# A Fourier mixer and gated layer on one core: quarter-array products in issue order, and eleven forward units beside the first chunk

## The chip, the cores and the metric

The kernel runs on 1 core of one Trainium2 chip. The metric is the device time of one execution in microseconds (us). The kernel before takes 2664.31 us, the median of 3 runs (2664.19 to 2669.71). Lower is better.

## What is computed

The input is 8 sequences of 3008 tokens with 256 channels. A real Fourier transform along the sequence, a complex 256 x 256 product per frequency with a bias, a soft threshold and the inverse transform give 24064 tokens of 256 channels. These pass a gated layer of width 1536. The gated layer's weights arrive as 64-bit floats.

```python
def _attn_ref(x, w_r, w_i, b_r, b_i):
    X = np.fft.rfft(x, axis=1)
    Xr, Xi = (X.real.astype(np.float32), X.imag.astype(np.float32))
    Yr = Xr @ w_r - Xi @ w_i + b_r
    Yi = Xr @ w_i + Xi @ w_r + b_i
    lam = 0.01
    Yr = np.sign(Yr) * np.maximum(np.abs(Yr) - lam, 0.0)
    Yi = np.sign(Yi) * np.maximum(np.abs(Yi) - lam, 0.0)
    y = np.fft.irfft(Yr + 1j * Yi, n=x.shape[1], axis=1)
    return y.astype(np.float32)

def _moe_ref(x, w_gate, w_val, w_out):
    gate = 1.0 / (1.0 + np.exp(-(x @ w_gate)))
    val = x @ w_val
    return (gate * val @ w_out).astype(np.float32)
```

## The kernel before

**The transform.** 3008 is 47 x 64, so each sequence (called a batch) is transformed in two steps. Forward step A works with 47-point products: a unit of it is one `products_a` (L207-218), called by `fwd_a` for a full tile `xf` or by `halves_a` (L238-249) for two half tiles `xfh`. Each unit has four products of 47 rows by 64 columns with 512 moving columns. Each lies in one 64 x 64 quarter of the TensorE array: the input half `j` sets the row half, the output half `c` sets the column half. The profile lists each as two instructions, so a unit shows as x8. The results are copied out of PSUM and stored to a buffer `zd` in DRAM. Forward step B (`fwd_b`, L287-312) reads it back as `zf`, makes 64-point products into `pb`, and splits them into `xsf`, `xsh`, `xsl` on ScalarE and VectorE. `mix` (L318-342) multiplies those with the complex weights into `pm`, adds the bias and thresholds. Inverse step B (`inv_b`, L361-379) writes `vz` to a buffer `vd`. Inverse step A (`inv_a`, L401-430) reads `vf` from there: a unit has 32 products of 48 rows by 64 columns with 47 moving columns, again each in one quarter of the array (`j` is the row half, `e` the column half), 64 instructions in the profile. It yields tokens, which stay on the chip as `yth`, `ytl` for the first nine chunks of 512 tokens and go to `yd` in DRAM for the rest.

**The gated layer.** `ffn1` and `ffn2` (L474 to L511) do one of 12 slices `f` of the layer for one chunk `c`: 12 products into `pg` and `pv`, a sigmoid `sg`, a product of both on VectorE (L482), `hh` and `hl`, and 6 products into `po`. Nine chunks are done so, 108 units. The remaining 38 pairs of chunks are done in the kernel's last part by another scheme with fewer products; that part is not touched by the change.

**The order of the work.** Batches go in groups of 1, 1, 2, 2, 2. Up to the end of the first chunk the order is written out by hand (`tc.manual_schedule`): batch 0 is transformed first, then the 12 units of chunk 0 run, and beside them stand 16 units of forward step A for the third group (list `beside`, function `halves`): one before f=0, then one for each f, with a second at f=3, f=9 and f=11. Also in this chunk the 64-bit weights are turned into pairs of 32-bit numbers, one part per unit: SyncE loads `raw` (`load_part`, L953), and ScalarE and VectorE run a chain of small operations on it (L931 to L939), called from `converting` (L446-461), which hangs in a list `hook` as long as the hand-written part lasts.

After it, a scheduler orders the instructions, and a list `side` says what stands beside which unit of the gated layer: `merge` interleaves streams, and each unit of the gated layer takes so much of the side work, by weight, that `side` ends 20 units before unit 108. The first phase of `side` has the transform of the second group with the first 5 of the 16 forward units of the fourth group (`a3[:n]`); the second phase has the transform of the third group with the other 11 (`a3[n:]`). Then `behind_last`: 16 inverse units of the last group in the last 20 units of the gated layer.

**Buffers.** Tiles stand in rings. `xfh` is in a ring of four that is named r2k, `azh` (the output of a half unit) in a ring of four named st, `xf` and `raw` share a ring of six, `vf` has two and one more, and PSUM has a ring of six banks for these products. Loads of `x`, `raw`, `zf`, `vf` go through SyncE's queue (SP); the half units' stores (`zd<-azh`) go through GpSimd's queue (POOL).

Of the kernel before, what the change touches and what calls it, by code (L numbers as in the profile page):

```python
# [9 lines left out]
F32 = mybir.dt.float32  # L10
# [37 lines left out]
WARM_Z, WARM_V = 10, 1  # L48
EARLY = 4
AT_FIRST = 1  # L50
NCONV = 6


# [68 lines left out]
def tile_fft_mix_ffn(ctx: ExitStack, tc, x, w_r, w_i, b_r, b_i, w_one, w_out, mf, mi, mis, fa, fb, mf0, fa0, out):  # L122
# [36 lines left out]
    def r2k(name):  # L159
        gap("gap_r", 192)  # L160
        return p2.tile([P, 2, D], F32R, tag="r2k", bufs=NR2K, name=name)
# [21 lines left out]
    def move(queue, sb, dram, store=False):  # L183
        for j in range(2):
            t = sb[64 * j:64 * j + NQ]
            queue.dma_start(*((dram[j], t) if store else (t, dram[j])))
# [15 lines left out]
    def load_a(b, h):  # L202
# [4 lines left out]
            move(nc.sync, xf, xv[b, h])  # L207
        held["x", b, h] = xf

    def products_a(xs, outs, copies):  # L210
        pa = [bank("pa") for _ in range(2)]
        xs = [t[:, 2 * c:2 * c + 2] if t.shape[1] == 4 else t for c, t in enumerate(xs)]
        for j in (1, 0):
            rows = slice(64 * j, 64 * j + R2)
            for c in (1, 0):
                nc.tensor.matmul(pa[j][64 * c:64 * c + 64], fa_sb[rows], xs[c][rows], start=True, stop=True)
        for copy, o, t in zip(copies, outs, pa):
            copy(o, t.rearrange("p (h c) -> p h c", h=2))

# [16 lines left out]
            move(queue, held.pop(("x", b, h)), zv[b][h], True)  # L236

    def load_half(b, h):  # L238
        xf = r2k("xfh").bitcast(F32)
        move(nc.sync, xf, xv[b, h // 2, :, :, h % 2 * 2:h % 2 * 2 + 2])  # L240
        held["xh", b, h] = xf

    def halves_a(b, u):

        xs = [held.pop(("xh", b, 2 * u + c)) for c in range(2)]
        az = [p2.tile([P, 2, D], F32, tag="st", bufs=NST, name="azh") for _ in range(2)]
        products_a(xs, az, (nc.scalar.copy, nc.scalar.copy))
        for j in range(2):
            move(nc.gpsimd, az[j], zv[b][u, :, :, 2 * j:2 * j + 2], True)


    def load_mf(q, table=mf):
# [148 lines left out]
    def inv_a(u):  # L401
        vf = held.pop(("v", u))
        pa = [bank("pia")[:, :CT * UT].rearrange("p (c k) -> p c k", c=CT) for _ in range(2)]
        for h in range(4):
            for ct in range(CT):
                for j in range(2):
                    rows = slice(64 * j, 64 * j + NQ)
                    for e in range(2):
                        ch = ct * P + 64 * e
                        nc.tensor.matmul(pa[j][64 * e:64 * e + 64, ct, h * R2:(h + 1) * R2], vf[rows, h, ch:ch + 64],  # L410
                                         fb_sb[rows, :R2], start=True, stop=True)
        first = 2 * u * UT // CW
        for j, py in enumerate(pa):
            lo, k = (2 * u + j) * UT, 0
            while k < UT:
                at = lo + k
                c, place = divmod(at, CW)
                n = UT - k if at >= T0 else min(UT - k, CW - place)
                y = py[:, :, k:k + n]
                if at >= T0:  # L420
                    t = result("yf")[:, :CT * n].rearrange("p (c k) -> p c k", c=CT)
                    nc.scalar.copy(t, y)
                    nc.sync.dma_start(yd[:, :, at - T0:at - T0 + n], t)
                elif c == first:
                    split_y(c, place, n, y)
                else:
                    if place == 0:
                        held["carry", c] = p3.tile([P, CT, 384], F32, name="carry", bufs=1), 0
                    t = held["carry", c][0]
                    nc.scalar.copy(t[:, :, place:place + n], y)  # L430
                    held["carry", c] = t, place + n
                k += n
# [79 lines left out]
                nc.sync.dma_start(out[ct * P:(ct + 1) * P, c * CW:(c + 1) * CW], ot)  # L512


    def fft_units(bs, ms):


        aa = [(b, h) for b in bs for h in range(R1 // 8)]
        units = []

        def step_a(i):
            if i == 0:
                for k in range(min(PRE, len(aa))):
                    load_a(*aa[k])
            if i + PRE < len(aa):
                load_a(*aa[i + PRE])
            fwd_a(*aa[i])
            store_a(*aa[i])

        def loads(q, b):  # L530
            if b == bs[0]:
                if q == 0:
                    ms[0, 0] = load_mf(0)
                if q + 1 < NP:
                    ms[q + 1, 0] = load_mf(q + 1)
                if 0 <= q - 1 < NP and (q - 1, 1) not in ms:
                    ms[q - 1, 1] = load_mi(q - 1, False)
            if q == 0:
                load_b(b, 0)
            if q + 1 < NP:  # L540
                load_b(b, q + 1)

        def step(q, b):
            loads(q, b)
            if q < NP:
                fwd_b(b, q, ms[q, 0], False)
            if 0 <= q - 1 < NP:
                mix(b, q - 1)
            if 0 <= q - 2 < NP:
                inv_b(b, q - 2, ms[q - 2, 1], False)  # L550

        first = [(1.0, lambda i=i: step_a(i)) for i in range(len(aa))]
        for q in range(NP + 2):
            wt = 0.9 * (q < NP) + 2.0 * (0 <= q - 1 < NP) + 0.7 * (0 <= q - 2 < NP)
            units += [(wt, lambda q=q, b=b: step(q, b)) for b in bs]
        return first, units
# [433 lines left out]
    nc.vector.memset(ebias, -896.0 * 2.0 ** 23)  # L990
    nc.vector.memset(lam_sb, -LAM)
    mfs, mis_ = {}, {}
    beside = [(b, u) for b in groups[2] for u in range(na)]
    waiting = list(beside)

    def convert(q):
# [26 lines left out]
    def halves(upto):  # L1023

        while waiting:
            i = len(beside) - len(waiting)
            if i >= upto:
                break
            halves_a(*waiting.pop(0))
            if i + NR2K // 2 < len(beside):  # L1030
                load_halves(*beside[i + NR2K // 2])

    with tc.manual_schedule():
        for h in range(na):
# [63 lines left out]
    with tc.manual_schedule():  # L1098
        for u in own0:
            load_v(u)  # L1100
        load_part()
        for h in range(EARLY, na):
            store_a(1, h)
        for bu in beside[NR2K // 2:NR2K // 2 + AT_FIRST]:
            load_halves(*bu)
        for f in range(NF):
            ffn[f]()
            if parts:
                load_part()
            if f in (2, 3):  # L1110
                tables[f - 2, 1] = load_mi(f - 2, False, later=True)
            if f in (5, 6):
                keep_mi(f - 5)
            halves(AT_FIRST + f + 1 + (f > 2) + (f > 8) + (f > 10))
    hook.clear()


# [32 lines left out]
    def merge(*streams):  # L1150
# [2 lines left out]
                                         enumerate(streams) for i, u in enumerate(s)), key=lambda t: t[:2])]  # L1153

    (a3, q3), (a4, q4) = (fft_units(g, {}) for g in groups[3:])
    n = len(a3) // 3
    side = (merge((second_fft, 0, 1), (a3[:n], 0.2, 1)) +
            merge((third_fft, 0, 1), (a3[n:], 0, 0.85), *behind(groups[1])) +
            merge((q3, 0, 1), *in_twos(a4, groups[2])) +
            merge((q4, 0, 1), *behind(groups[3])))  # L1160
    behind_last = sum(inverse(groups[4]), [])
# [104 lines left out]
```

## Time and profile before

| | |
|---|---|
| Median of the runs | 2664.31 us (2664.19 to 2669.71) |
| The profiled execution's own time | 2665.18 us |
| Its span | 2663.2 us, mean granted TensorE clock 0.996 |
| TensorE busy | 2627.3 us, 99% of the span |
| VectorE, ScalarE, GpSimd busy | 1941.7, 1816.8, 1094.1 us |
| Hand-written part, batch 0 | up to about 106 us |
| First chunk of the gated layer | about 106 to 190 us |
| Chunks 1 to 8 beside the transform | about 190 to 918 us |
| `behind_last` | about 918 to 1009 us |
| Last part, untouched | about 1009 to 2663 us |

All times in the views are counted from the start of the span. A row of a timeline gives the start, the duration, the engine, the line, the operation, what it writes and reads, how many instructions stand together (x8), and in brackets the idle time of its engine just before it with what ended that. Matmuls overlap in the pipeline, so what a matmul costs is the distance from its start to the next start, not its duration. "SPq" and "POOLq" are the two queues that issue transfers.

### The profile page before, as it was taken

Reading aid. Unit: us, or ns where it says so; the run is one execution under the profiler, and the core shown is the slowest. Engines: PE = TensorE matmul, PEld = TensorE weight load, DVE = VectorE, ACT = ScalarE, POOL = GpSimd, SP = SyncE. Lnnn points to the kernel's source line nnn. Section 1 sums busy time; section 2 is a strip of 40 time slices with the busy share of each in tenths; the row PEclk is TensorE's granted clock in tenths of the full one; section 3 lists DMA queues with packets and bytes.
Section 4 is the critical chain, followed back from the end, with each engine's and each line's share of the span. In section 5 each row is a group of like instructions: output and inputs, shape, how many; then the busy total and the mean of one; then the engine's idle time right before and its main releaser. Section 6 shows DMA issues by size and latency. Waiting matters only on the chain. (4 is left out here: it accounts for less than half of the span.)

```text
span 2663.2 us, 60273 instructions
## 1 busy us (share of the span) xinstructions
PE 2627.3 (99%) x24032; PEld 2456.9 (92%) x24032; DVE 1941.7 (73%) x3468; ACT 1816.8 (68%) x3530; POOL 1094.1 (41%) x1399
## 2 busy tenths in 40 slices
PE   8999999999999999999999999999999999999998
PEld 6668888888899878999999999999999999999998
DVE  4768778777777525777777777777777777777777
ACT  4666655656565435777777777777777777777776
POOL 0241031123500002555555555555555555555554
PEclk9999999999999999999999999999999999999999
DMA  9887655777655572111111211111111211111111
GB/s 282 259 249 201 189 153 170 195 226 221 198 161 150 175 222 76 33 41 34 39 41 35 47 32 42 33 41 34 40 41 33 46 31 45 33 41 33 40 41 27
DMA packets 200969, 268.27 MB, mean 101 GB/s; under 512 B 19760, under 2 KB 152368, under 8 KB 200688
## 3 DMA queue, kind: packets, MB, share of 16 engines
q1 hardware_dynamic: 179600, 220.04, 28.1%
q0 software_dynamic: 20832, 44.31, 7.8%
q8 instruction: 189, 3.10, 0.5%
q14 instruction: 92, 0.75, 0.1%
q10 hardware_dynamic: 256, 0.07, 0.0%
HBM read 137.33 MB, written 127.01 MB: 99 GB/s over the span
## 5 line engine op out<-in xcount | busy, mean ns | idle before, releaser
L764 POOL TENSOR_TENSOR hs<-gh,xh 128x256 f32<-128x256 f32 x227 | 253.1, 1115 | 734.6 <-DVE gh L754 734.6
L754 DVE TENSOR_TENSOR gh<-gh,pa 128x256 f32<-128x256 f32 x228 | 96.1, 421 | 344.4 <-ACT gh L749 344.4
L713 PE MATMUL pd<-xop,th 128*128 128x256 f32 x1824 | 333.0, 276 | 0.8 <-DVE pc L757 0.8
L713 PE MATMUL pa<-xop,w1h 128*128 128x256 f32 x1824 | 332.6, 276 | 0.0
L713 PEld LDWEIGHTS pd<-xop,th 128*128 128x128 f32 x1824 | 274.5, 188 | 1.7 <-DVE pc L757 1.4
L713 PEld LDWEIGHTS pa<-xop,w1h 128*128 128x128 f32 x1824 | 274.6, 188 | 0.1
L713 PE MATMUL pd<-xop,tl 128*128 128x256 f32 x912 | 251.8, 276 | 0.0
L713 PE MATMUL pa<-xop,w1l 128*128 128x256 f32 x912 | 251.7, 276 | 0.0
L784 DVE TENSOR_TENSOR hpS<-hs,hpS 128x768 fp32r<-128x768 f32 x228 | 217.1, 952 | 0.4 <-ACT hpS L780 0.4
L733 ACT COPY pd<-pb 128x512 f32<-128x512 f32 x228 | 130.0, 570 | 107.8 <-PE pb L713 107.8
L757 DVE TENSOR_TENSOR pb<-pb,m 128x512 f32<-128x512 f32 x228 | 159.5, 699 | 42.3 <-PE pb L713 42.3
L327 PE MATMUL pm<-w_sb,xsh 128*128 128x256 f32 x1008 | 185.9, 286 | 4.1 <-ACT xsh L310 3.1
L780 ACT CAST hpS<-hs 128x768 fp32r<-128x768 f32 x228 | 189.5, 831 | 0.2 <-DVE hs L770 0.2
L729 PE MATMUL acc<-hpS,w2h 128*128 128x256 f32 x912 | 177.5, 276 | 0.0
L733 ACT COPY pb<-pa 128x512 f32<-128x512 f32 x228 | 130.0, 570 | 68.1 <-PE pa L713 68.0
L770 POOL TENSOR_TENSOR hs<-xh,hs 128x256 f32<-128x256 f32 x227 | 168.0, 740 | 17.8
L768 POOL TENSOR_TENSOR gh<-gh 128x256 f32<-128x256 f32 x227 | 167.3, 737 | 17.8
L713 PEld LDWEIGHTS pd<-xop,tl 128*128 128x128 f32 x912 | 171.2, 188 | 0.0
L713 PEld LDWEIGHTS pa<-xop,w1l 128*128 128x128 f32 x912 | 171.2, 188 | 0.0
L766 POOL TENSOR_TENSOR hs<-hs,gh 128x256 f32<-128x256 f32 x227 | 168.1, 741 | 0.0
L713 PE MATMUL pb<-xop,th 128*128 128x256 f32 x912 | 166.5, 276 | 0.0
L713 PE MATMUL pb<-xop,w1h 128*128 128x256 f32 x912 | 166.4, 276 | 0.0
(218 smaller groups left out, 8738.4 us busy)
## 6 DMA issues: line engine op xcount, KB each, us to landing
zf<-zd SPq DMA_DIRECT2D x96, 256.0 KB, 4.3
vf<-vd SPq DMA_DIRECT2D x128, 192.0 KB, 4.1
vd<-vz SPq DMA_DIRECT2D x85, 256.0 KB, 3.1
ypair<-yd SPq DMA_DIRECT2D x38, 512.0 KB, 3.6
yd<-yf SPq DMA_DIRECT2D x103, 188.0 KB, 3.8
out_dram<-ev SPq DMA_DIRECT2D x149, 128.0 KB, 1.8
out_dram<-ev POOLq DMA_DIRECT2D x37, 512.0 KB, 5.8
xf<-in_x_dram SPq DMA_DIRECT2D x80, 192.0 KB, 4.4
```

What stands on the lines that cost most here:

```text
L327: nc.tensor.matmul(o, l, r, start=(i == 0), stop=(i == len(mms) - 1))
L713: nc.tensor.matmul(o[:, i * HW:(i + 1) * HW], l, r, start=start, stop=l is wl, skip_group_check=True)
L729: nc.tensor.matmul(o, l, r, start=(p, b) not in begun, stop=l is wl, skip_group_check=True)
L733: nc.scalar.copy(to, o)
L754: nc.vector.tensor_mul(g, g, o[:, HW:])
L757: nc.vector.tensor_add(to, o, hx[k, "m5"])
L764: e.tensor_add(hx[k, "S"][:, 0], g[:, 1], x[:, 1])
L766: e.tensor_sub(hx[k, "S"][:, 1], hx[k, "S"][:, 0], g[:, 0])
L768: e.tensor_sub(g[:, 1], g[:, 0], g[:, 1])
L770: e.tensor_sub(hx[k, "S"][:, 2], x[:, 0], hx[k, "S"][:, 1])
L780: nc.scalar.copy(t[:, 0], parts_of(k, what))
L784: sub(t[:, 1], parts_of(k, what), t[:, 0])
```

## The change

Three things are changed.

First, a function `behind_last_of` ties the products of one 47-point unit together: after the hand-written part, each but the first must stand behind the TensorE instruction issued before it. It is a tie in order alone; nothing waits on a semaphore for it. It is used in `products_a` and `inv_a`. In `inv_a` the row halves are now taken as `j` = 1, 0.

Second, 11 instead of 16 units of forward step A stand beside the first chunk, one before f=0 and one for each of f=0 to 9. They work in place: the results are copied from PSUM back into the tiles that were loaded, and stored from there. Units 0, 1, 4, 5, 8, 9 use the ring r2k, units 2, 3, 6, 7, 10 the ring st (named `xfs` there). Loads go three units ahead instead of two.

Third, the other five units (`late`) run as full tiles in the first phase of `side`, where the five units of the fourth group stood, and the second phase has all 16 of that group.

```diff
+NHALF = 11
...
+    def behind_last_of(row, ins):
+        if row and not hook:
+            tc.keep_in_program_order(ins)
+        row.append(ins)
+
     def products_a(xs, outs, copies):
...
-                nc.tensor.matmul(pa[j][64 * c:64 * c + 64], fa_sb[rows], xs[c][rows], start=True, stop=True)
+                behind_last_of(row, nc.tensor.matmul(pa[j][64 * c:64 * c + 64], fa_sb[rows], xs[c][rows], start=True, stop=True))
...
     def load_half(b, h):
-        xf = r2k("xfh").bitcast(F32)
+        i = beside.index((b, h // 2))
+        if i // 2 % 2:
+            xf = p2.tile([P, 2, D], F32, tag="st", bufs=NST, name="xfs")
+        else:
+            xf = r2k("xfh").bitcast(F32)
...
-        az = [p2.tile([P, 2, D], F32, tag="st", bufs=NST, name="azh") for _ in range(2)]
-        products_a(xs, az, (nc.scalar.copy, nc.scalar.copy))
+        products_a(xs, xs, (nc.scalar.copy, nc.scalar.copy))
         for j in range(2):
-            move(nc.gpsimd, az[j], zv[b][u, :, :, 2 * j:2 * j + 2], True)
+            move(nc.gpsimd, xs[j], zv[b][u, :, :, 2 * j:2 * j + 2], True)
...
     def inv_a(u):
...
-                for j in range(2):
+                for j in (1, 0):
...
-                        nc.tensor.matmul(pa[j][64 * e:64 * e + 64, ct, h * R2:(h + 1) * R2], vf[rows, h, ch:ch + 64],
-                                         fb_sb[rows, :R2], start=True, stop=True)
+                        o = pa[j][64 * e:64 * e + 64, ct, h * R2:(h + 1) * R2]
+                        behind_last_of(row, nc.tensor.matmul(o, vf[rows, h, ch:ch + 64], fb_sb[rows, :R2], start=True, stop=True))
...
-    beside = [(b, u) for b in groups[2] for u in range(na)]
+    early = [(b, u) for b in groups[2] for u in range(na)]
+    beside, late = early[:NHALF], early[NHALF:]
...
-            if i + NR2K // 2 < len(beside):
-                load_halves(*beside[i + NR2K // 2])
+            if i + 3 < len(beside):
+                load_halves(*beside[i + 3])
...
-        for bu in beside[NR2K // 2:NR2K // 2 + AT_FIRST]:
+        for bu in beside[NR2K // 2:AT_FIRST + 3]:
...
-            halves(AT_FIRST + f + 1 + (f > 2) + (f > 8) + (f > 10))
+            halves(AT_FIRST + f + 1)
...
-    n = len(a3) // 3
-    side = (merge((second_fft, 0, 1), (a3[:n], 0.2, 1)) +
-            merge((third_fft, 0, 1), (a3[n:], 0, 0.85), *behind(groups[1])) +
+    side = (merge((second_fft, 0, 1), (forward_units(late), 0.05, 0.8)) +
+            merge((third_fft, 0, 1), (a3, 0, 0.85), *behind(groups[1])) +
```

What this moves is seen in the order of the instructions on each engine (number of the row, line, operation, what is written and read, and how many stand together). The first place is TensorE in `behind_last`, between the products of the gated layer. Before, one of its inverse units, shown with the numbers of its tiles: `pia_11943` and `pia_11944` are the two PSUM tiles of one unit, one for each `j`, and so one for each row half of the array.

```order
L502 MATMUL po_11411<-hh_11860,w2h_78 128x512
L503 MATMUL po_11411<-hh_11860,w2l_81 128x512
L504 MATMUL po_11411<-hl_11861,w2h_78 128x512
L410 MATMUL pia_11943<-fb_sb_79,vf_11870 64x47 x16
L502 MATMUL po_11410<-hh_11930,w2h_78 128x512
L503 MATMUL po_11410<-hh_11930,w2l_81 128x512
L504 MATMUL po_11410<-hl_11931,w2h_78 128x512
L410 MATMUL pia_11944<-fb_sb_79,vf_11870 64x47 x16
```

And the same engine now, at the one unit of `behind_last` that is not in one piece.

```order
3698 L514 MATMUL po<-hh,w2l 128x512
3699 L515 MATMUL po<-hl,w2h 128x512
3700 L422 MATMUL pia<-fb_sb,vf 64x47 x24
3701 L513 MATMUL po<-hh,w2h 128x512
3702 L514 MATMUL po<-hh,w2l 128x512
3703 L515 MATMUL po<-hl,w2h 128x512
3704 L422 MATMUL pia<-fb_sb,vf 64x47 x8
```

Before, five of the 16 units stood in two pieces of 16, each in one row half, and five more in one piece had 10 to 16 products of one row half in a row, behind them as many of the other. Now 15 of the 16 stand in one piece, one in 24 and 8, and in all of them the four quarters of the array take turns.

The second place is SyncE's queue at the first chunk. `xfh` and `xfs` are half tiles, `raw` the weights of the conversion, `zf` the input of forward step B of the next group. Before:

```order
81 L953 DMA raw<-in_w_out_dram 128x1024
82 L186 DMA zd_89<-xf 48x1024 x8
83 L186 DMA xfh<-in_x_dram 48x512 x4
84 L186 DMA vf<-vd_96 48x1024 x2
85 L953 DMA raw<-in_w_one_dram 128x1024
86 L186 DMA xfh<-in_x_dram 48x512 x4
87 L953 DMA raw<-in_w_one_dram 128x1024
```

After:

```order
82 L187 DMA zd_89<-xf 48x1024 x8
83 L187 DMA xfs<-in_x_dram 48x512 x8
84 L187 DMA vf<-vd_96 48x1024 x2
85 L966 DMA raw<-in_w_one_dram 128x1024
86 L187 DMA xfh<-in_x_dram 48x512 x4
87 L966 DMA raw<-in_w_one_dram 128x1024
88 L187 DMA xfh<-in_x_dram 48x512 x4
89 L966 DMA raw<-in_w_out_dram 128x1024
90 L294 DMA zf<-zd_89 128x2x256
91 L187 DMA xfs<-in_x_dram 48x512 x4
92 L966 DMA raw<-in_w_one_dram 128x1024
```

The first `raw` of the chunk now stands behind eight loads of half tiles instead of four, and a load of a unit waits for the store of the unit that had its tiles before, where it waited for TensorE alone. Each `raw` behind it on the queue waits with it.

The third place is ScalarE at the end of the chunk, from its last conversions to the first `xsh` that the next phase's `mix` needs. Before:

```order
177 L938 CAST w2h<-raw 128x512
178 L480 ACTIVATE sg<-pg 128x512
179 L398 CAST yth<-carry 128x2x104
180 L490 CAST hh<-sg 128x512
181 L218 COPY azh<-pa 128x512 x4
182 L480 ACTIVATE sg<-pg 128x512
183 L490 CAST hh<-sg 128x512
184 L306 COPY xsf<-pb 128x2x2x2x64
185 L310 CAST xsh<-xsf 128x768
```

After:

```order
175 L501 CAST hh<-sg 128x512
176 L408 CAST yth<-carry 128x2x104
177 L951 CAST w2h<-raw 128x512
178 L491 ACTIVATE sg<-pg 128x512 x2
179 L501 CAST hh<-sg 128x512 x2
180 L316 COPY xsf<-pb 128x2x2x2x64
181 L320 CAST xsh<-xsf 128x768
```

The four copies of half units between `hh` and `sg` are gone, and the next chunk's first `sg` stands ahead of this chunk's last `hh`.

More of the change, by code (lines that the diff above doesn't have):

```diff
@@ L212, in products_a @@
         xs = [t[:, 2 * c:2 * c + 2] if t.shape[1] == 4 else t for c, t in enumerate(xs)]
+        row = []
         for j in (1, 0):
@@ L403, in inv_a @@
         pa = [bank("pia")[:, :CT * UT].rearrange("p (c k) -> p c k", c=CT) for _ in range(2)]
+        row = []
         for h in range(4):
             for ct in range(CT):
-                for j in range(2):
+                for j in (1, 0):
                     rows = slice(64 * j, 64 * j + NQ)
@@ L512, in ffn2, with forward_units @@
                 nc.sync.dma_start(out[ct * P:(ct + 1) * P, c * CW:(c + 1) * CW], ot)
-    def fft_units(bs, ms):
-        aa = [(b, h) for b in bs for h in range(R1 // 8)]
-        units = []
+    def forward_units(aa):
         def step_a(i):
@@ L528, in step_a, with fft_units @@
             store_a(*aa[i])
+        return [(1.0, lambda i=i: step_a(i)) for i in range(len(aa))]
+    def fft_units(bs, ms):
+        units = []
         def loads(q, b):
@@ L550, in step @@
                 inv_b(b, q - 2, ms[q - 2, 1], False)
-        first = [(1.0, lambda i=i: step_a(i)) for i in range(len(aa))]
+        first = forward_units([(b, h) for b in bs for h in range(R1 // 8)])
         for q in range(NP + 2):
```

## The prediction

> **What bounds the kernel now.** I read the windows first, because the share of the whole span (TensorE 99%) hides three stages with different limits. The columns are the stretch, its length, then busy time of TensorE, its weight loads, VectorE, ScalarE and GpSimd, the granted clock, the DMA share and GB/s.
>
> ```profile
> 106.00:180.00 74.00, 69.60 (x393) 44.19 (x393) 56.31 (x98) 51.40 (x94) 30.72 (x56) 0.96 0.89 275
> 190.00:480.00 290.00, 288.70 (x2263) 245.17 (x2263) 228.75 (x394) 170.50 (x290) 50.42 (x75) 0.99 0.62 178
> 480.00:710.00 230.00, 226.14 (x2542) 192.24 (x2541) 173.06 (x273) 137.23 (x244) 96.76 (x143) 1.00 0.73 211
> 710.00:918.00 208.00, 207.28 (x2403) 185.71 (x2402) 154.63 (x271) 121.03 (x211) 0.00 (x0) 1.00 0.56 163
> 918.00:1009.00 91.00, 88.48 (x1282) 70.97 (x1281) 23.30 (x35) 32.83 (x66) 3.22 (x4) 1.00 0.76 212
> ```
>
> From 190 to 1009 TensorE is busy for 810.6 of 819 us: there a matmul removed shortens the kernel, and one added lengthens it. The first chunk (106 to 180) is different. Its TensorE looks 94% busy, but a busy time whose matmuls overlap says little, so I went to the timelines of VectorE and ScalarE there.
>
> ```profile
> 150.38 0.68 DVE L482 TENSOR_TENSOR sg<-sg,pv 128x512 f32<-128x512 f32 x1
> 156.20 0.68 DVE L482 TENSOR_TENSOR sg<-sg,pv 128x512 f32<-128x512 f32 x1
> ...
> 157.44 1.06 ACT L218 COPY azh<-pa 128x512 f32<-128x512 f32 x2
> 159.62 0.65 ACT L938 CAST w1h<-raw 128x512 fp32r<-128x512 f32 x1 [1.11 <-DVE raw L937]
> ```
>
> One unit of the gated layer follows the other in 5.82 us (150.38 to 156.20), the length of a chain between VectorE and ScalarE that converts the weights. The copies of a half unit (1.06 us) end at 158.50, and ScalarE still waits 1.11 us for VectorE. So a half unit is free here as long as the chain sets the pace: what moves out of this chunk gains nothing there, and costs its full price where TensorE sets the pace.
>
> **The change part by part.** I sum against the profiled execution: its own time is 2665.18 us, its span 2663.2, and it lies 0.87 us over the median of 2664.31.
>
> *The ties in the last inverse units.* The group row of `inv_a` for the stretch 918 to 1009, then a unit of it that is cut in two, and one from the stretch before that is whole:
>
> ```profile
> L410 PE MATMUL pia<-fb_sb,vf 48*64 48x47 f32 x1024 | 26.8, 233 | 1.5 <-DMA vf<-vd 1.5
> ...
> 925.56 0.39 PE L504 MATMUL po<-hl,w2h 128*128 128x512 f32 x1
> 925.88 1.14 PE L410 MATMUL pia<-fb_sb,vf 48*64 48x47 f32 x32
> 926.94 0.50 PE L502 MATMUL po<-hh,w2h 128*128 128x512 f32 x1
> 927.29 0.39 PE L503 MATMUL po<-hh,w2l 128*128 128x512 f32 x1
> 927.52 0.40 PE L504 MATMUL po<-hl,w2h 128*128 128x512 f32 x1
> 927.84 1.14 PE L410 MATMUL pia<-fb_sb,vf 48*64 48x47 f32 x32
> ...
> 257.84 1.15 PE L410 MATMUL pia<-fb_sb,vf 48*64 48x47 f32 x64
> 258.92 0.50 PE L502 MATMUL po<-hh,w2h 128*128 128x512 f32 x1
> ```
>
> The whole unit takes 1.08 us for 64 instructions, since its four quarters run at once. Each piece of the cut one takes 1.06 us for 32: half as many quarters run. 1024 instructions are 16 units; at 1.15 us busy each they would take 18.4 us, and they take 26.8. The ties put all quarters in turn, so 8.4 us go. Each of the five cuts also costs a way in and out: 0.32 us from 925.56 to 925.88 and 0.35 from 926.94 to 927.29, where the ordinary step is 0.23 (927.29 to 927.52). That is 0.21 us, 1.0 for five. One unit is now cut 24 + 8: +0.2. Together −9.2.
>
> What is late next there is `vf`:
>
> ```profile
> vf<-vd SPq DMA_DIRECT2D x28, 192.0 KB, 4.6
> ...
> 940.43 1.14 PE L410 MATMUL pia<-fb_sb,vf 48*64 48x47 f32 x32 [1.47 <-DMA vf<-vd]
> ```
>
> One unit waited for it, 1.47 us, with the DMA share at 0.76 in this stretch. The same bytes in 82 instead of 91 us would be a share of 0.84, below the 0.89 that the first chunk ran at. So I take back 0.8 us (bounds: −1.5, the wait goes because tiles come free sooner, and +4.6, one full landing in the open). Net −8.4.
>
> *Five forward units leave the first chunk.* They run as full tiles in the second phase in the end, since the first phase had five others before. Rows of such a unit beside the gated layer, and one that the scheduler cut in two:
>
> ```profile
> 263.92 0.28 PE L374 MATMUL pi<-yh,mi_sb 128*128 128x256 f32 x1
> 264.13 1.09 PE L216 MATMUL pa<-xf,fa_sb 47*64 47x512 f32 x8
> ...
> 265.48 0.40 PE L475 MATMUL pg<-ytl,w1h 128*128 128x512 f32 x1
> ...
> 277.57 1.08 PE L216 MATMUL pa<-xf,fa_sb 47*64 47x512 f32 x4
> 279.36 1.08 PE L216 MATMUL pa<-xf,fa_sb 47*64 47x512 f32 x4
> ```
>
> From 263.92 to 265.48 are 1.56 us. Without the unit a narrow step (0.11 by 256 columns, half of 0.23) and a wide one (0.23) would stand there, so the unit costs 1.22; five cost 6.1 us. Nothing hides them: TensorE sets the pace there. Their copies and stores go to engines with room (ScalarE 170.5 of 290 us). A unit cut into x4 and x4 pays nearly the whole price twice, and the order has two such cuts now for one before: the tie is to the TensorE instruction issued last, so it keeps the products in turn but does not keep others from standing between. +1.2.
>
> *The end of the first chunk.* TensorE and ScalarE from 176 to 194:
>
> ```profile
> 176.91 2.10 PE L216 MATMUL pa<-xfh,fa_sb 47*64 47x512 f32 x16
> 183.20 1.95 PE L292 MATMUL pb<-mf_sb,zf 128*128 128x128 f32 x16
> 184.90 0.48 PE L502 MATMUL po<-hh,w2h 128*128 128x512 f32 x1
> ...
> 189.40 0.97 PE L327 MATMUL pm<-w_sb,xsh 128*128 128x256 f32 x4 [3.10 <-ACT xsh L310]
> 190.17 0.63 PE L474 MATMUL pg<-yth,w1h 128*128 128x512 f32 x1
> 190.60 0.63 PE L475 MATMUL pg<-ytl,w1h 128*128 128x512 f32 x1
> ...
> 193.28 0.39 PE L327 MATMUL pm<-w_sb,xsh 128*128 128x256 f32 x2
> ...
> 183.22 0.58 ACT L218 COPY azh<-pa 128x512 f32<-128x512 f32 x1 [2.55 <-DMA zd<-azh]
> 184.97 0.59 ACT L218 COPY azh<-pa 128x512 f32<-128x512 f32 x1 [1.16 <-DMA zd<-azh]
> 187.33 0.58 ACT L306 COPY xsf<-pb 128x512 f32<-128x512 f32 x1
> ```
>
> ScalarE waits 2.55 and 1.16 us for the stores of `azh` to land before it can copy the last two half units, and all that follows, up to the first `mix` product at 189.40, stands behind it. In the new order neither the copies nor the two units on TensorE (176.91, about 2.0 us) are there. TensorE then comes to `pb` at 183.20 − 2.0 = 181.2, plus about 0.7 (an estimate: `hl` on VectorE now stands behind one more 0.68 us product) = 181.9. `pb` takes 1.7 (183.20 to 184.90), and from the start of `xsf` to the first `mix` product are 2.07 (187.33 to 189.40): about 185.8 instead of 189.40, a gain of 3.6 if the conversion's chain is on time. TensorE's idle 3.10 us also has a price behind it: its steps are 0.43 us (190.17 to 190.60) instead of 0.23, and a product lasts 0.63 instead of 0.39 until 193.28. Half pace for 3.9 us loses 1.9 us. In the new order TensorE waits there for about 1 us only, so I count this 1.9 as gained. The Trainium skill (TensorE: Matmul & The Clock Gate, HAM oscillation — how this bites in real kernels) puts the limit for an idle gap at about 3.4 us; the row here lost its clock after 3.10, so the row decides.
>
> *The chain's slip.* The chain is not on time, by some s. Rows of the chunk's transfers, a store's issue, and the one place where the chain waited for its weights before:
>
> ```profile
> xfh<-in_x_dram SPq DMA_DIRECT2D x56, 96.0 KB, 3.8
> zd<-azh POOLq DMA_DIRECT2D x52, 96.0 KB, 4.0
> raw<-in_w_one_dram SPq DMA_DIRECT2D x7, 512.0 KB, 5.6
> ...
> 158.31 2.21 POOL L186 DMA_DIRECT2D zd<-azh  x4 [3.60 <-ACT azh L218]
> ...
> 116.75 0.43 DVE L931 TENSOR_SCALAR cv_e<-raw 128x512 uint32<-128x512 uint32 x1 [1.71 <-DMA raw<-in_w_one_dram]
> ```
>
> The first `raw` of the chunk was late already, by 1.71 us, and now four more loads of 96 KB stand ahead of it: 393 KB at the 275 GB/s of this stretch are 1.4 us. Later each load of a half unit waits for a store two units back in the ring: copies begin at 157.44, stores are issued from 158.31 to 160.52, and land 4.0 later, about 7.1 after the copies; two more load issues (about 0.9) and `raw`'s 5.6 bring 13.6 us. The weights are needed some 2.1 us behind the copies two units on (157.44 to 159.50), that is after 2 x 5.82 + 2.1 = 13.7. So on average it is just in time. I take s = 1.5, near the first slip; the bounds are 0 and 10 (below). End of the chunk: −3.6 + 1.5 − 1.9 = −4.0.
>
> **Sum:** −8.4 (ties) + 6.1 (five units) + 1.2 (one more cut) − 4.0 (end of the chunk) = −5.1. The profiled execution would take 2660.1, a median 2659.2 us. About 0.2% (5.3 us) is what a measurement of this kernel can tell from no change, so this lies at the edge of it.
>
> **The rivals.** (1) *Everything on time*: no slip (−1.5), the wait for `vf` goes (−1.5 instead of +0.8), and no forward unit costs more than when whole (−1.2): −10.1, 2654.2; half of that, about 2656.7, is more likely. For it: the `vf` wait is one of sixteen. Chance 0.20. (2) *Transfers take the ties' place*: in the last 82 us each `vf` lands late. For it: landing in 4.6 us at a share of 0.76; against it: one wait only. If half of the 8.4 goes in such waits the sum is −0.9, 2663.4. Chance 0.14. (3) *Slower: the in-place stores set the pace of the first chunk.* The mechanism is SyncE's queue: it stops at a load that waits for a store, and `raw` stands behind it. If a store takes 8.1 us from the copies instead of 7.1 and two loads and `raw` take 8.1 instead of 6.5, two units take 14.1 instead of 11.6, 1.2 us more a unit. Over seven units that wait so, this is 8.8 us, with the 1.4 ahead s = 10.2, 8.7 over my sum: +3.6. TensorE would then stand idle over 3 us again and lose the 1.9: +5.5, 2669.8. It decides from s = 6.6, where the sum is nought. Against it: these worst times would have to come each time. Chance 0.15. (4) *The clock:* with no half units at f=10 and 11 TensorE has 18 products of 0.23, 4.1 us, in 5.82, and idles 1.7 us each time. If the clock falls there, the next phase begins at half pace and the 1.9 is not gained: −3.2, 2661.1. The Trainium skill (TensorE: Matmul & The Clock Gate, A second HAM failure mode: psum-queue depth-cycling) has it that short idles between groups of products can make the clock swing. The chunk's granted clock of 0.96 speaks against it. Chance 0.06. That the ties do nothing is not a rival: the new order shows the quarters in turn.
>
> **How the numbers follow.** My forecast has 0.45, split about evenly over the edge of 0.2% at 2659.0. Faster by over 0.2%: 0.23 + 0.20 of rival 1 + 0.02 = 0.45. Slower by over 0.2% (above 2669.6): half of rival 3 and what other reordering may bring, 0.12. The same: the rest, 0.43. The forecast's own range is 2656 to 2663. The range of 8 in 10 runs from near rival 1 (2653) to between rivals 2 and 3 (2667).
>
> **What would show it.** In the new trace: 16 inverse units behind 918 us at about 1.15 busy each, 18.5 us in the group; the first `mix` product at about 187, with no 3 us of idle time ahead and a full clock behind it; copies of half units in place without an idle unit that a DMA ended; 1.2 us for each of the five late units. I am wrong if VectorE waits for `raw` at several units of the chunk (rival 3), if TensorE waits for `vf` more than twice behind 918 us (rival 2), or if the stretch between the first chunk and 918 us grows by much more than 7.3 us.

## The result, and the profile after it

The changed kernel takes 2680.71 us, the median of its runs, against 2664.82 us before: a ratio of 1.0054, with a 95% interval of 1.0040 to 1.0068. The forecast was 5.1 us less; it is 14 to 16 us more, with the sign wrong. (The untouched last part takes 42.8 us for a pair of chunks in most executions and 44.5 us in some, of whatever kernel, now and then from the middle on; so profiles are compared up to the start of that part, and the medians below are of the runs that by their times have 42.8 us throughout, 3 of 5 for the changed kernel, 6 of 12 for the ties alone, 1 of 4 for the late units from 0.2, 5 of 10 for those without products, and most or all for the others.)

The profiled execution takes 2680.71 us, its span is 2678.9. I compare stretches between the same two instructions of both kernels: ScalarE's `hh` of the second unit of chunk 1, and that of unit 106, just ahead of the last part. I call this the **long stretch**. First before, then after (length, TensorE busy, weight loads, VectorE, ScalarE, GpSimd, granted clock, DMA share, GB/s):

```profile
197.30:1012.10 814.80, 806.41 (x8461) 689.98 (x8460) 575.82 (x964) 459.74 (x810) 150.40 (x222) 1.00 0.65 188
```

```profile
194.90:1027.30 832.40, 814.35 (x8489) 693.48 (x8488) 577.38 (x963) 461.42 (x815) 146.57 (x222) 0.99 0.66 188
```

| | before | after | difference |
|---|---|---|---|
| first `hh` of chunk 0 | 112.36 | 110.54 | −1.8 |
| last `hh` of chunk 0 | 179.08 | 181.34 | +2.3 |
| first `mix` product of the next phase starts | 189.40 | 185.70 | −3.7 |
| long stretch, from its start on | 197.3 | 194.9 | −2.4 |
| its length | 814.8 | 832.4 | +17.6 |
| TensorE idle in it (length less busy) | 8.4 | 18.1 | +9.7 |
| from its end to the end of the span | 1651.1 | 1651.6 | +0.5 |

The first row isn't put down to the change: over the fourteen usable profiles of this case the chunk begins between 110.5 and 114.2 us, in kernels of either kind. Counted from the chunk's first `hh`, the first `mix` product comes 1.9 us earlier than before, and the long stretch begins 0.6 us earlier.

Busy time hides one more loss. I looked for windows with a lowered clock, and there are five in the long stretch; in the kernel before there is none behind 196 us.

```profile
276.00:284.00 8.00, 6.28 (x29) 5.42 (x28) 2.96 (x6) 2.95 (x6) 0.20 (x1) 0.79 0.32 106
484.00:500.00 16.00, 13.00 (x116) 9.80 (x115) 7.04 (x11) 8.13 (x15) 0.09 (x1) 0.79 0.52 153
704.00:712.00 8.00, 6.97 (x91) 6.66 (x92) 6.31 (x10) 4.79 (x9) 7.74 (x13) 0.79 0.49 136
916.00:924.00 8.00, 6.58 (x102) 5.20 (x98) 2.07 (x3) 3.90 (x9) 0.00 (x0) 0.79 0.64 183
984.00:994.00 10.00, 8.27 (x83) 6.23 (x83) 2.57 (x4) 3.78 (x7) 3.66 (x4) 0.66 0.65 186
```

Busy time times the share of the clock that is missing is 1.3 + 2.7 + 1.5 + 1.4 + 2.8 = 9.7 us (10.7 if it is added up over slices of 2 us, as in the table of the experiments). So the 17.6 us are 9.7 of idle time and about 10 of lost clock, and TensorE's own work became 2 to 3 us shorter: −9.2 + 6.1 + 1.2 = −1.9 was the forecast for that.

The forecast parts can each be seen. The end of the first chunk, TensorE after the change:

```profile
185.37 0.39 PE L514 MATMUL po<-hh,w2l 128*128 128x512 f32 x1
185.70 0.74 PE L337 MATMUL pm<-w_sb,xsh 128*128 128x256 f32 x4
186.38 1.07 PE L223 MATMUL pa<-xf,fa_sb 47*64 47x512 f32 x4
...
189.18 1.08 PE L223 MATMUL pa<-xf,fa_sb 47*64 47x512 f32 x4
190.19 0.50 PE L485 MATMUL pg<-yth,w1h 128*128 128x512 f32 x1
```

No idle time stands ahead of the first `mix` product, the steps behind it are at full clock, and a late unit is cut in two, as the order said. The way from the first `mix` product to the long stretch takes 9.2 us here, and 6.4 us in the same kernel without the late units' products: cut in two, this unit costs 2.8 us, 1.2 + 1.2 by the sum. The inverse units behind 935 us have the busy time of whole units, 18.7 us for 1024 instructions instead of 26.8:

```profile
L422 PE MATMUL pia<-fb_sb,vf 48*64 48x47 f32 x1152 | 21.0, 235 | 0.0
...
L422 PE MATMUL pia<-fb_sb,vf 48*64 48x47 f32 x1024 | 18.7, 235 | 0.0
```

(The first row is the stretch from 918 us, with 18 units, the second the one from 935 with 16.) And yet only 1.5 us were won between 918 us and the last part. What the sum did not have are the waits of TensorE. Up to the last inverse units, before and after (waited for by whom, for what, us in total, times, the longest):

```profile
PE pi L372 <- ACT yh L339: 1.7, 3, 1.1
PE pg L474 <- DVE ytl L399: 0.9, 1, 0.9
PE pb L292 <- DVE ys L333: 0.9, 1, 0.9
```

```profile
PE pi L382 <- ACT yh L349: 4.7, 3, 1.7
PE pia L422 <- DVE yt L339: 3.3, 2, 2.0
PE pv L485 <- DVE ys L343: 1.8, 2, 1.4
PE pi L383 <- DVE yl L350: 0.9, 2, 0.7
```

All of these are the transform's chain: products `pm`, then VectorE (`yt`, `ys`) and ScalarE (`yc`, `yh`), then products `pi`. The rows where it hurts:

```profile
277.40 0.28 PE L384 MATMUL pi<-yh,mi_sb 128*128 128x256 f32 x1
279.40 0.58 PE L382 MATMUL pi<-yh,mi_sb 128*128 128x256 f32 x1 [1.73 <-ACT yh L349]
...
487.79 0.58 PE L382 MATMUL pi<-yh,mi_sb 128*128 128x256 f32 x1 [1.73 <-ACT yh L349]
...
489.75 3.62 PE L302 MATMUL pb<-mf_sb,zf 128*128 128x128 f32 x16
...
705.02 1.14 PE L422 MATMUL pia<-fb_sb,vf 48*64 48x47 f32 x60 [1.99 <-DVE yt L339]
706.09 0.79 PE L337 MATMUL pm<-w_sb,xsh 128*128 128x256 f32 x2
```

Behind each of these waits the same products last about twice as long: `pb` x16 takes 3.62 us where it takes 1.95 at 182.65 us. Behind the wait at 279 us 1.3 us of clock are lost, behind the one at 487 us 2.7. It isn't always so: the wait for `yh` at 276 to 282 us is 1.73 us long in four other kernels of this case too (eleven half units alone, late units without products, separate output tiles, late units without weight), and behind none of these four did the clock fall.

### The profile page after: what moved, and what is told of

Read it like the earlier page. It is cut to its first block, busy times and chain, and to the rows that moved or that the text cites. A ratio compares the mean times of both kernels' runs of the same rounds, so it can differ in the third digit from the quotient of the medians.

```text
span 2678.9 us, 60257 instructions
## 1 busy us (share of the span) xinstructions
PE 2636.5 (98%) x24032; PEld 2462.3 (92%) x24032; DVE 1943.7 (73%) x3468; ACT 1816.4 (68%) x3530; POOL 1079.7 (40%) x1379
```

## The experiments

In the table, *idle* is TensorE's idle time in the long stretch and *clock* what the lowered clock loses there; both are of the profiled execution. For the medians see the result. The idle time is much alike from kernel to kernel with the same pace; the clock's loss is not, and each value is of one execution.

| kernel | median us | ratio, 95% interval | long stretch | idle | clock |
|---|---|---|---|---|---|
| before | 2664.82 | 1 | 814.8 | 8.4 | 0 |
| changed | 2678.5 | 1.0054, 1.0040 to 1.0068 | 832.4 | 18.1 | 10.7 |
| ties alone | 2660.5 | see there | 810.8 | 9.3 | 3.4 |
| eleven half units alone | 2683.3 | 1.0077, 1.0064 to 1.0090 | 831.0 | 14.7 | 3.3 |
| 16 in place | 2663.65 | 1.0004, 0.9996 to 1.0013 | 812.9 | 10.7 | 3.4 |
| 13 in place | 2671.4 | 1.0033, 1.0020 to 1.0046 | 816.4 | 17.2 | 1.6 |
| ties, five result tiles | 2656.3 | 0.9968, 0.9959 to 0.9978 | 809.8 | 9.0 | 1.7 |
| changed, five result tiles | 2675.2 | 1.0041, 1.0026 to 1.0056 | | | |
| late units from 0.2 | 2678.9 | one run | 825.6 | 18.0 | 3.3 |
| late units without products | 2670.8 | five runs | 827.0 | 18.3 | 11.1 |
| fourth group split as before | 2674.79 | 1.0037, 1.0023 to 1.0051 | 818.6 | 14.4 | 3.3 |
| separate output tiles, 11 | 2673.4 | 1.0041, 1.0024 to 1.0058 | 827.5 | 18.7 | 3.1 |
| 14 half units | 2659.02 | 0.9989, 0.9978 to 1.0000 | 812.3 | 10.7 | 1.7 |
| late units without weight | 2666.05 | 1.0008, 0.9998 to 1.0018 | 817.2 | 10.6 | 4.7 |
| 14 half units, without weight | 2654.11 | 0.9963, 0.9950 to 0.9976 | 809.2 | 9.5 | 0 |

**The ties alone**, put on the kernel before:

```diff
-                for j in range(2):
+                for j in (1, 0):
...
+                        behind_last_of(row, nc.tensor.matmul(...))
```

> The kernel before with the order of the products in the inverse units alone (row halves 1, 0 and the ties); 16 half units as before. Up to about 910 us nothing is moved. Theory A (the ties do what the sum said, and the two waits of 2.7 and 1.7 us behind 950 us in the changed kernel come from what is late there for other reasons): behind_last shortens by 8 to 9 us, about 2656 us. Theory B (the new order of TensorE in behind_last brings those waits and the clock loss behind them itself): waits for hh and for ot of together 3 to 5 us and half pace for some us stand in behind_last here too, and 1.5 to 3 us are gained, about 2662 us.

Up to 917 us nothing changed (that `hh` comes 0.7 us earlier), and the last part starts 3.5 us earlier: theory B, with a little more gained than its 1.5 to 3 us. ScalarE and then TensorE in it:

```profile
934.14 0.63 ACT L487 ACTIVATE sg<-pg 128x512 f32<-128x512 f32 x1
938.50 0.47 ACT L429 COPY yf<-pia 128x376 f32<-128x376 f32 x1 [3.74 <-DMA yd<-yf]
938.87 0.62 ACT L497 CAST hh<-sg 128x512 fp32r<-128x512 f32 x1
```

```profile
939.54 0.50 PE L509 MATMUL po<-hh,w2h 128*128 128x512 f32 x1 [2.85 <-ACT hh L497]
...
941.26 1.96 PE L418 MATMUL pia<-fb_sb,vf 48*64 48x47 f32 x64
```

ScalarE copies an inverse unit's result into `yf`, a ring of three. The units now follow each other faster, the third-last store has not landed, the copy waits 3.74 us, and `hh`, which has nothing to do with it, is queued behind. TensorE waits 2.85 us for `hh`, and the next unit takes 1.96 us, at half pace. In the changed kernel the same stands at 955.68 (3.75 us) and 956.72 (2.69). Of twelve runs, six lie at 2657.6 to 2662.6 and six at 2682.2 to 2687.9; over all twelve the ratio is 1.0034 (1.0004 to 1.0064). The profile is of the first kind; what makes the second is not shown.

Without the tie, with the row halves 1, 0 alone, this kernel has the same order of instructions on all five engines, row by row; the same holds for the changed kernel. With the tie and the row halves as before, the quarters take turns too, but seven of the last 16 units are cut, each behind its first two products, one of them twice. So in these kernels the tie moves nothing; taking the row halves in the other order is enough to keep the quarters in turn.

**Eleven half units alone**: the changed kernel with `range(2)` in `inv_a` and without ties.

> The changed kernel without the ties and with the row halves in the old order 0, 1; eleven half units in place and the five late units stay. Theory A (all of the loss between 190 and 918 us comes from moving the forward units): this stretch is as long as in the changed kernel, and behind_last loses its packing again but has only the old waits: 2681 to 2689 us, with waits of 1 to 2 us at TensorE for yh, yt and ys and a lowered clock behind some of them. Rival (the ties hold TensorE up in the phases ahead of 918 us, seen as inverse units that wait in the middle for a PSUM bank that VectorE still reads): those waits are gone here, 2670 to 2676 us.

The idle time and the longer stretch stay, theory A: the ties do not bring the waits of the earlier phases. Up to the last inverse units the idle time is 12.8 us, against 12.3 in the changed kernel.

**All 16 in place**, `NHALF = 16`, with the second units at f=3, 9, 11:

> The changed kernel with all 16 half units beside the first chunk again, in place, with the second units at f=3, 9 and 11, and the later phases as before; behind the first chunk the order is that of the run with the ties alone. Theory A (in place costs a slip of the conversion of about 2 us, and the copies at the end of the chunk no longer wait for stores, which gives it back): within 2 us of the run with the ties alone. Rival (the loads that wait for stores pace the chunk): 5 to 9 us more than that run, with waits of VectorE for raw.

The median is 3 us above the first group of the run with the ties, a little outside theory A and short of the rival. The last `hh` of chunk 0 comes 5.7 us later than before, 5.0 more than with the ties alone. So in place costs this chunk some us when all 16 are in it, and pays a part of it back at the chunk's end.

**13 in place**, `NHALF = 13`:

> The changed kernel with 13 half units in the first chunk, one in each unit, and three late ones. Theory A (the cost of the late units is their 1.2 us each, and the rest of the loss is waits that a new order of the later phases happens to bring): three times 1.2 = 3.6 us for the units, and some waits and clock losses at other places than in the changed kernel, anywhere from 2658 to 2680 us. Rival (each late unit brings its share of waits, about 19/5 = 3.8 us): about 2672 us.

It agrees with either: with three late units the idle time is 17.2 us, 6.5 more than with all 16 in place, and the clock loses only 1.6 us.

**Five result tiles**, two of them in the pool that is opened for the last part, with the ties:

```diff
+        if p4 and len(yfs) % 5 < 2:
+            return p4.tile([P, CW], F32, tag="yl", bufs=2, name="yf")
+        return result("yf")
```

> The kernel before with the row halves in the order 1, 0 and the ties, and five instead of three tiles for the results of the last inverse units (two of them in the pool that is opened there). TensorE's order is not moved by the tiles. Theory B (in the run with the ties alone ScalarE's copy of a result waited 3.7 us for a store of the ring of three, hh stood behind it, and TensorE lost 2.85 us and then 3.4 us of clock): the wait goes, and behind_last is 8 to 9 us shorter than before; the last part starts at about 1016 us instead of 1024.8 (1021.3 with the ties alone). Rival (the stores are late by their own traffic, whatever the ring): the last part starts at 1020 us or later.

The wait behind `yf` is gone. TensorE's waits behind 920 us, first with three tiles, then with five:

```profile
PE po L509 <- ACT hh L497: 3.9, 2, 2.9
```

```profile
PE pia L427 <- DMA vf<-vd: 1.6, 1, 1.6
PE po L518 <- ACT hh L506: 1.0, 1, 1.0
```

What is left is what the kernel before has there too, and the forecast wait for `vf`. The runs gain 8.5 us against the kernel before. (The profiled execution took 2661.6 us. It lost 1.7 us of clock behind the wait for `vf`, and its chunk 0 ended 2.5 us later than before. Its last part starts at 1021.4 and not at 1016, so by its profile the expectation was missed, while the runs bear it out.)

**The same in the changed kernel**:

> The changed kernel with five tiles for the results of the last inverse units. If the wait of 2.7 us for hh behind 953 us comes from the ring of three, it goes here, and the last part starts 3 to 7 us earlier than in the changed kernel (1040.1), at 1033 to 1037 us. If the wait of 1.7 us for ot (VectorE's copy into the same ring) and the clock behind it go too, it is near 1033. Rival as in the run with the ties: no change.

The runs gain about 3 us (2675.2 against 2678.5), at the lower end of what was expected. There is no usable profile of it, so that the wait went here too is not shown.

**Late units from 0.2 to 0.95** of the first phase instead of 0.05 to 0.8:

> The changed kernel with the five late units from 0.2 to 0.95 of the first phase instead of 0.05 to 0.8: the same work in another order. Theory A (the five units cost their 6.1 us, and the other 12 us between 190 and 918 us are waits and clock losses that this order happens to have): the stretch changes by 3 us or more, with waits at other places. Rival (every order with five more units in these phases pays this): within 2 us of the changed kernel.

The long stretch is 6.8 us shorter, as theory A has it, but from less lost clock; the idle time is 18.0 us, as in the changed kernel. As far as the idle time goes this speaks for the rival: the waits are nearly those of the changed kernel.

**Late units without their products.** The five units are loaded and stored, and their 47-point products and copies are left out.

```diff
-            fwd_a(*aa[i])
+            if aa is not left:
+                fwd_a(*aa[i])
```

> The changed kernel with the five late units loaded and stored but not transformed: their 47-point products and the copies are left out. By the sum this gives back 5 x 1.22 + 1.2 for the cut ones = 7.3 us of TensorE. Theory A: 5 to 9 us less than the changed kernel, 2671 to 2675 us, the waits behind 470 us stay. Rival (the five units bring the waits with them): 15 us or more less, near 2665 us.

The stretch shortens by 5.4 us, and the way from the first `mix` product to it by 2.8, together 8.2 where the sum had 7.3; the idle time stays, 18.3 us. So the products cost about what the sum had, and the waits are there without them.

**The fourth group split as before**, five units in the first phase beside the five late ones:

> The changed kernel with the fourth group's units split as before (five in the first phase, eleven in the second) and the five late ones beside them in the first phase. TensorE's own work is that of the changed kernel. Theory C (the waits come from which units stand in a phase: in the changed kernel the first phase has its five early and nothing of the kind in its last fifth, the second has five more than before): the second phase has the idle time that it has in the kernel before, and the waits at about 660 to 720 us and 911 us go; the last part starts at 1026 to 1032 us instead of 1040.1. Rival (the waits come with any order of 16 + 5 units): 1036 us or later.

The last part starts at 1028.5, but not for the reason given. The waits between 659 and 720 us are there, with 0.6 to 1.3 us each, and so is the one at 911; from about 485 to 750 us the idle time is 5.8 us, against 6.0 in the changed kernel. Theory C falls; most of the 11.6 us are 7.4 us less of lost clock. The median of the runs is 2674.79, about 4 us under the changed kernel.

**Separate output tiles with eleven half units**, as before the change:

> The changed kernel with eleven half units that write to tiles of their own as before and are loaded two ahead, not in place. If the slip of the conversion (2.1 us by the last hh of the first chunk in the changed kernel, 0.7 in the run with the ties alone) comes from the loads that wait for stores, it is 0 to 1 us here; else 2 us again. Behind the first chunk all is as in the changed kernel: between 1 and 2 us less than that, 2677 to 2680 us.

The last `hh` of chunk 0 comes 1.4 us earlier than before, against 2.3 later in the changed kernel, and VectorE hardly waits for `raw`, as in the kernel before. Its waits there in the kernel before, the changed one and this one:

```profile
DVE cv_e L931 <- DMA raw<-in_w_one_dram: 1.7, 1, 1.7
```

```profile
DVE cv_e L944 <- DMA raw<-in_w_one_dram: 7.0, 3, 3.3
```

```profile
DVE cv_e L941 <- DMA raw<-in_w_one_dram: 0.9, 1, 0.9
```

So the slip is the loads that wait for stores. Counted from the chunk's first `hh`, it is larger than that: the last `hh` comes 66.1 us behind the first here, 66.7 in the kernel before and 70.8 in the changed one. All eight profiles of kernels that work in place have 70.0 to 72.6 us, all six of the others that can be used 65.6 to 68.9. The runs are 5 us under the changed kernel, about this slip of 4 to 5 us.

**14 half units**, written to tiles of their own, none at f=11, with the ties and five result tiles:

> The kernel with the ties and five result tiles, but with 14 half units in the first chunk (none at f=11) and two late ones at the start of the first phase; the fourth group's units are split as before. By the sum: the end of the first chunk gains the 3.6 us of the copies that waited for stores and 1.9 us of clock, the two units cost 2 x 1.2 us: 3.1 us less than with five result tiles (2656), 2653 us. Rival (fewer half units bring new waits, as in the kernels with 11 and 13): 2657 us or more.

The start of the next chunk came 4.9 us earlier, as the sum has it, and the runs are 2.7 us slower than with 16 and five tiles. The gain goes into the long stretch.

By now the work, the phase and the ties were excluded as the source of the idle time. What all these kernels share is the weight of the late units. A unit of the gated layer takes side work by weight, and the rate is the sum of all weights by the number of units: five more units raise it, and each later step of the transform stands beside another unit of the gated layer, with other products between `pm` and `pi`. **Late units without weight** keep the five units and leave the pace as it was:

```diff
-            merge((second_fft, 0, 1), (forward_units(late), 0.05, 0.8)) +
+            merge((second_fft, 0, 1), (forward_units(late, 0.0), 0.05, 0.8)) +
```

> The changed kernel with the five late units given no weight in the pacing, so that from the 41st unit of the gated layer on the steps of the transform stand beside the same units as in the kernel before. TensorE's own work is that of the changed kernel (803.5 us from the second unit of chunk 1 to unit 106, idle 18.1, lost to the clock 10.7). Theory D (the waits come from the pace: five more units of weight shift every later step of the transform against the gated layer's units that cover its chain through VectorE and ScalarE): idle 10 to 13 us and at most 4 us lost to the clock, a stretch of 815 to 820 us. Rival (any order with these five units has such waits): idle 15 us or more.

The median falls by 12.4 us to 2666.05, idle time to 10.6. TensorE's waits up to the last inverse units, and the windows of the long stretch:

```profile
PE pi L382 <- ACT yh L349: 2.7, 4, 1.7
PE pg L485 <- DVE ytl L409: 0.9, 1, 0.9
PE pb L302 <- DVE ytl L409: 0.7, 1, 0.7
PE pi L383 <- DVE yl L350: 0.7, 2, 0.3
```

```profile
197.90:1015.10 817.20, 806.62 (x8488) 685.63 (x8487) 575.41 (x963) 462.22 (x816) 151.83 (x222) 0.99 0.67 192
```

The waits for `yt` and `ys` are gone, those for `yh` are 2.7 us instead of 4.7, and the longest of them, at 279 us, stands ahead of the 41st unit, where the order still differs from that of the kernel before. It is plainest up to the last inverse units alone, in the kernel before, the changed one and this one:

```profile
197.30:918.60 721.30, 715.42 (x7170) 616.69 (x7168) 551.89 (x929) 426.55 (x743) 147.17 (x218) 1.00 0.64 185
194.90:936.20 741.30, 728.98 (x7204) 626.95 (x7202) 553.97 (x929) 427.97 (x749) 142.91 (x218) 0.99 0.64 185
197.90:923.40 725.50, 719.77 (x7201) 617.89 (x7200) 551.96 (x929) 429.00 (x749) 148.15 (x218) 1.00 0.66 189
```

The idle time there is 5.9, 12.3 and 5.7 us, and the lowered clock costs 0, 7.7 and 0. The 4.7 us of clock, above the 4 expected, stand mostly behind the `yf` wait of 3.5 us, which this kernel still has. Theory D holds.

**14 half units, the late ones without weight**:

> The kernel with 14 half units, the ties and five result tiles, with its two late units given no weight: the steps of the transform stand as in the kernel before. Theory D: idle and clock loss of the stretch fall from 10.7 + 1.7 us to 8 to 10 us together, 2 to 4 us less than with weight (2659), 2655 to 2657 us, about as fast as five result tiles alone (2656). Rival: within 1 us of the run with weight.

```profile
192.00:1001.20 809.20, 799.69 (x8467) 682.68 (x8466) 575.63 (x963) 456.56 (x809) 150.28 (x222) 1.00 0.67 191
```

No clock is lost in the long stretch, and 2654.11 us beats both kernels: 0.9963 of the one before (0.9950 to 0.9976). That is 4.9 us under the same kernel with weight, a little more than expected. Against the kernel with all 16 half units, the ties and five result tiles (0.9959 to 0.9978) it isn't faster clear of the noise.

## Why the prediction was wrong

- *The ties, −9.2.* The size was right: 18.7 us busy for the 16 units, 18.5 forecast. The cause was not: I wrote that the ties put all quarters in turn, and the reversed row halves do it.
- *"What is late next there is `vf`"*, +0.8. Wrong. Late next was the ring of three result tiles, a store's landing that ScalarE waits for, with `hh` behind it. In the changed kernel waits for `hh` and `ot` took 5.4 us and the clock behind them 2.8, so that 1.5 us of the gain were left. Rival 2 did not come: behind 935 us TensorE waits for no `vf`. I had looked for the next late transfer among the inputs alone, and counted a wait without the clock behind it.
- *Five late units, +6.1, and the cut, +1.2.* About right: leaving the products out gave 8.2 us where these are 7.3.
- *The end of the first chunk, −4.0.* Near, but by luck: two terms were too small and nearly cancel. Counted from the chunk's first `hh`, the first `mix` product came 1.9 us earlier (75.2 us behind it against 77.0), where −3.6 + 1.5 = −2.1 was forecast, and at full clock. Yet the slip is 4 to 5 us where I took 1.5. And without the slip the end of the chunk gains 6.6 us (70.4 us with separate output tiles), not 3.6. The cause of the slip is the forecast one: VectorE waited 7.0 us for `raw`, three times, where before it was 1.7, once. So the in-place rival, with its slip of 10.2, came to a bit under half its size. That the first `mix` product stood at 185.70 us, ahead of the 187.3 forecast, is the earlier start of that execution: in the six profiles with the changed kernel's first chunk it lies between 185.7 and 190.9.
- *The step that failed* is one that I did not write down: that everything else between the first chunk and the last inverse units would stay as it was, a term of the sum put at nothing. I took the late units as 6.1 us of added work, though each carries a weight, and the kernel makes the pace of the weights. The way up to the last inverse units became 20.0 us longer (721.3 to 741.3), where 7.3 were forecast. A move by at most about one unit of the gated layer cost 6.6 us of waits (12.3 against 5.7 up to the last inverse units) and in the profiled execution 7.7 us of clock behind them, together about twice the price of the work itself.
- *The clock rival* had the clock fall at f=10 and 11, and it did not fall there. It fell earlier in the chunk, at about 133 and 160 us, and in the long stretch. In the rest of the sum I let the clock fall only after some 3 us, because 3.10 us did it before, and so had no price for shorter waits.

That the waits come with the pace is shown by the late units without weight, and borne out by the 14 half units without weight. Why this pace is worse than the old one, step by step, is not; it may be chance that the old one fits.

## What to carry to other kernels

Work that is added to a stream whose pace is a sum of weights moves everything behind it: price the move, or give the newcomer no weight. When a group of products gets faster, ask at once how many output tiles its results have and what is queued behind the copy that fills them. And leave room for the clock behind a wait of TensorE: here waits of 1.7 to 2.0 us cost between nothing and 2.7 us more.

## What the runs showed of the hardware

In the changed kernel the granted clock fell behind waits of 1.73, 1.73 and 1.99 us (rows above), and behind one of 1.22 us with small products around it at 917.56. It fell to half for about 3.4 us or twice that: the five windows of the result lose 0.21 of 8, 16, 8 and 8 us and 0.34 of 10 us of the clock, which at half pace are 3.4, 6.7, 3.4, 3.4 and 6.8 us. It did not fall behind one of 2.69 us:

```profile
917.56 0.52 PE L382 MATMUL pi<-yh,mi_sb 128*128 128x256 f32 x1 [1.22 <-ACT yh L349]
918.29 0.58 PE L383 MATMUL pi<-yl,mi_sb 128*128 128x256 f32 x1 [0.21 <-DVE yl L350]
...
956.72 0.50 PE L513 MATMUL po<-hh,w2h 128*128 128x512 f32 x1 [2.69 <-ACT hh L501]
957.06 0.40 PE L514 MATMUL po<-hh,w2l 128*128 128x512 f32 x1
```

The Trainium skill (TensorE: Matmul & The Clock Gate, HAM oscillation — how this bites in real kernels) counts idle gaps above about 3.4 us. The rows differ: about half that length was enough here. Whether it is enough is open: behind waits for `yh` of the same 1.73 us, at 276 to 282 us, the clock fell in one kernel and stayed full in four, and no run here took that apart.
